# Retention followed by a maxout feed-forward: weights converted in pairs, another order of the first chunks, weight sums one tile earlier, and a last store in two halves

## The chip, the cores and the metric

The kernel runs on one core of one Trainium2 chip. The metric is the device time of one execution in microseconds (us). A kernel's figure is the median of its executions. Differences of one or two microseconds are read from ratios over several rounds, and their 95% intervals are given.

## The reference

The reference is retention (attention with a decay mask instead of a softmax), followed by a feed-forward layer that takes the maximum of three products.

```python
# q, k, v: 8 batches x 8 heads x 576 positions x 64, float32
scores = q @ k.T / 8
gamma  = 1 - 2.0 ** (-5 - arange(8))                  # one per head
D      = where(i >= j, gamma ** (i - j), 0)           # decay and causal mask
x      = ((scores * D) @ v)  as 4608 rows x 512
h      = maximum(maximum(x @ w1, x @ w2), x @ w3)     # 512 -> 768
out    = h @ w_out                                    # 768 -> 512
# w1, w2, w3, w_out arrive as float64
```

## The kernel before

The rows are worked off in 36 chunks of 128 rows for the retention and in 9 tiles of 512 rows for the feed-forward. The retention of the next tile is interleaved with the feed-forward of the present one. Tile 0 uses plain matmuls. Tiles 1 to 8 use a scheme of seven products instead of eight, which needs sums of weight blocks ("weight sums") and sums of hidden blocks.

Each chunk goes through three steps. The step `transposes` puts q and k with the head dimension on the partitions. The step `scores` multiplies them, masks on VectorE, and updates the running state. The step `values` multiplies by v and by the state. The chunks up to 7 are transposed by TensorE and copied out of PSUM by ScalarE. From chunk 8 on VectorE transposes, and for this the kernel loads the data in blocks of 32, by 32 small loads:

```python
def load(g):
    rows = (("k", k), ("q", q), ("v", v)) if g < BY_PE else (("k", k), ("v", v))
    for n, src in () if g < BY_PE else (("q", q), ("kx", k)):
        ...                                    # 4 x 4 loads of 16 KB for each of q and kx
    for n, src in rows:
        ...                                    # one load of 256 KB each
```

The float64 weights come as 24 pieces of 128x512 (512 KB each), six loads ahead. Each piece is converted by bit operations: two masks on VectorE (expo, frac), three activations on ScalarE, two more VectorE steps (whole, and the sign joined to the exponent), and one multiply on GpSimd, which gives the weight. A generator cuts this into steps, and `convert(n)` emits the next n steps in the program between other work. Each engine works off its instructions in program order, so the place of a step in the program matters (in the changed kernel GpSimd once stands 6.0 us before an operation whose data have not landed, and a multiply whose inputs are there waits behind it).

```python
last = None
for n, piece in enumerate(pieces):
    high, expo, mant, frac = yield from masks(bits.pop(piece))   # masks of piece n
    if last:
        product(*last)                                           # then the end of piece n-1
        yield
    whole(mant, frac)
    yield
    last = piece, high, expo, mant
    ...
```

The beginning of the program, and where tile 0 and tile 1 emit conversions and weight sums:

```python
warm(6); load(0); load(1)
nc.sync.dma_start(gs[:], state_decay); nc.sync.dma_start(gq[:], out_decay)
load(2); load(3); load_weights(2); load(4); load_weights(4)
decay_values(0); transposes(0); warm(3); decay_values(1); scores(0); transposes(1)
values(0); decay_values(2); scores(1); transposes(2); values(1); decay_values(3); scores(2)
convert(2); transposes(3); values(2); convert(2); scores(3); ...

# ffn(t)
if t == 0:
    up_plain(t, h, fb, i)               # 4 matmul passes, then copy or maximum
    convert(4 if i > 0 else 8 if fp == 1 else 6)
...
if t == 1:
    weight_sums(n + 5)
...
for n in [[0], [1], [2], [3, 4]][m]:    # in tile 0's four down-products
    weight_sums(n)
```

## Time and profile before

The median was 834.87 us of the first three executions. The column "where" names the view of the profile; the list of TensorE's waits stands in the prediction.

| what | value | where |
|---|---|---|
| span of the profiled execution | 834.0 us | first line of the page |
| TensorE busy | 823.8 us, 99% | busy time by engine |
| last matmul to the end of the span | 3.56 us | timeline |
| VectorE, ScalarE, GpSimd busy | 51%, 21%, 22% | busy time by engine |

TensorE is the bound. The other engines matter only at the few places where TensorE waits for them, nearly all in the first tile, while the weights are being converted.

### The profile page before, as it was taken

The page shows a single profiled execution, that of the slowest core. Times are in us where ns is not written, and L with a number is a line of the kernel's source. Part 1 is how long each engine was busy: PE and PEld are TensorE (multiplying, and loading weights), DVE is VectorE, ACT ScalarE, POOL GpSimd, SP SyncE. Part 2 cuts the span into 40 slices and gives each one's busy share as a digit, 9 for nine tenths or more (in the row PEclk, how much of TensorE's full clock was granted, in tenths as well). Part 3 has the DMA queues.
Part 4 walks back from the last instruction along what each step waited for, and adds up shares of the span by engine and source line. Part 5 has one row for each costly group of instructions (what it writes and reads, how often), then busy time and mean ns, then how long its engine had stood idle before and what let it go on. Part 6 is the DMA issues. An engine that isn't in the chain of part 4 may idle for free.

```text
span 834.0 us, 12632 instructions
## 1 busy us (share of the span) xinstructions
PE 823.8 (99%) x4626; PEld 670.5 (80%) x4626; DVE 427.3 (51%) x803; ACT 174.7 (21%) x395; POOL 186.7 (22%) x182
## 2 busy tenths in 40 slices
PE   8899999999999999999999999999999999999998
PEld 8545556788888888888888888888888888888887
DVE  3879946754355443554444445544545435533341
ACT  2656721111111101111111111111111011111211
POOL 3535545511211130212011111111111202201000
PEclk9999999999999999999999999999999999999999
DMA  8946521334133323332233313332333223201001
GB/s 220 283 131 188 133 58 40 57 56 84 50 55 56 56 59 65 67 56 55 60 55 73 67 48 56 57 57 80 56 57 54 59 60 73 48 13 38 1 1 50
DMA packets 232509, 59.06 MB, mean 71 GB/s; under 512 B 213504, under 2 KB 230912, under 8 KB 232448
## 3 DMA queue, kind: packets, MB, share of 16 engines
q1 hardware_dynamic: 232304, 58.26, 31.1%
q8 instruction: 36, 0.59, 0.3%
q14 instruction: 25, 0.20, 0.1%
q10 hardware_dynamic: 144, 0.00, 0.0%
HBM read 48.76 MB, written 9.44 MB: 70 GB/s over the span
## 4 chain that ended last, share of the span: by engine, by line
PE 95%; DMA 2%; DVE 1%; SPq 1%; ACT 0%; POOL 0%; issue 0%; DVEq 0%
PE x L435 30%; PE z L435 15%; PE dx L311 10%; PE y L435 7%; PE up L493 7%; PE dz L311 5%; PE s L183 4%; PE o L213 4%; PE o L218 4%; PE kv L194 4%; PE dy L311 2%; PE down L484 2%; SPq L152 1%; DMA bits<-in_moe_w_dram 1%; DMA gs<-in_state_decay_dram 1%; SPq L146 1%
## 5 line engine op out<-in xcount | busy, mean ns | idle before, releaser
L435 PE MATMUL x<-S,T 128*128 128x256 f32 x576 | 147.9, 379 | 0.0
L435 PEld LDWEIGHTS x<-S,T 128*128 128x128 f32 x576 | 109.1, 190 | 15.4 <-ACT p L440 0.3
L156 POOL TENSOR_TENSOR vd<-vraw,gk 128x512 f32<-128x512 f32 x36 | 37.8, 1049 | 344.9 <-DMA vraw<-in_v_dram 319.4
L435 PE MATMUL x<-S,w 128*128 128x256 f32 x288 | 74.5, 381 | 1.2 <-DVE h L465 1.2
L435 PE MATMUL x<-xT,w 128*128 128x256 f32 x288 | 74.8, 382 | 0.0
L435 PE MATMUL z<-S,w 128*128 128x256 f32 x288 | 73.9, 379 | 0.0
L435 PE MATMUL z<-xT,T 128*128 128x256 f32 x288 | 73.9, 379 | 0.0
L435 PE MATMUL y<-xT,w 128*128 128x256 f32 x288 | 73.9, 379 | 0.0
L465 DVE TENSOR_TENSOR tmp<-x,p 128x256 f32<-128x256 f32 x48 | 20.4, 425 | 103.4 <-PE x L435 103.4
L440 ACT COPY p<-x 128x256 f32<-128x256 f32 x72 | 26.8, 372 | 221.0 <-PE x L435 221.0
L186 DVE TENSOR_TENSOR st<-s,causal 128x512 f32<-128x512 f32 x72 | 46.3, 685 | 44.6 <-PE s L183 44.6
L493 PE MATMUL up<-xT,w 128*128 128x512 f32 x144 | 63.8, 595 | 1.4 <-POOL w L387 1.4
L435 PEld LDWEIGHTS x<-S,w 128*128 128x128 f32 x288 | 49.3, 189 | 14.8 <-DVE h L465 1.8
L435 PEld LDWEIGHTS z<-S,w 128*128 128x128 f32 x288 | 54.7, 190 | 7.4
L435 PEld LDWEIGHTS y<-xT,w 128*128 128x128 f32 x288 | 54.7, 190 | 7.4
L435 PEld LDWEIGHTS z<-xT,T 128*128 128x128 f32 x288 | 54.3, 189 | 7.9
L220 DVE TENSOR_TENSOR xT<-o,gq 128x512 f32<-128x512 f32 x36 | 24.8, 690 | 67.9 <-PE o L218 62.4
L435 PEld LDWEIGHTS x<-xT,w 128*128 128x128 f32 x288 | 51.5, 190 | 6.6 <-issue 0.8
L493 PEld LDWEIGHTS up<-xT,w 128*128 128x128 f32 x144 | 26.6, 190 | 32.2 <-issue 29.9
L294 POOL TENSOR_TENSOR H<-h 128x256 f32<-128x256 f32 x24 | 18.1, 756 | 150.7 <-DVE h L478 150.0
L440 ACT COPY u<-x 128x256 f32<-128x256 f32 x72 | 26.8, 372 | 99.8 <-PE x L435 97.1
L183 PEld LDWEIGHTS s<-qT,kT 64*128 64x128 f32 x576 | 35.0, 187 | 15.6 <-issue 11.7
(92 smaller groups left out, 1210.1 us busy)
## 6 DMA issues: line engine op xcount, KB each, us to landing
bits<-in_moe_w_dram SPq DMA_DIRECT2D x18, 512.0 KB, 4.7
out_dram<-osb SPq DMA_DIRECT2D x36, 256.0 KB, 2.1
kraw<-in_k_dram SPq DMA_DIRECT2D x32, 256.0 KB, 3.0
vraw<-in_v_dram SPq DMA_DIRECT2D x32, 256.0 KB, 3.5
qraw<-in_q_dram SPq DMA_DIRECT2D x448, 16.0 KB, 1.8
kxraw<-in_k_dram SPq DMA_DIRECT2D x448, 16.0 KB, 1.8
bits<-in_moe_w_out_dram SPq DMA_DIRECT2D x6, 512.0 KB, 3.4
qraw<-in_q_dram SPq DMA_DIRECT2D x7, 256.0 KB, 4.4
```

What stands on the lines that cost most here:

```text
L156: nc.gpsimd.tensor_tensor(t[:], raws.pop(("v", g))[:], gk[:].unsqueeze(2).to_broadcast([C, H, D]), op=ALU.mult)
L183: nc.tensor.matmul(s[j][:, p, :], lhsT=kT[r, p, :], rhs=qT[r, p, :], start=True, stop=True)
L186: nc.vector.tensor_tensor(st[:, j], s[j][:], masks[start_of(g)][:].unsqueeze(1).to_broadcast([C, NP, C]), op=ALU.mult)
L194: nc.tensor.matmul(kv[:, p, :], lhsT=pair(kr, p)[r:], rhs=pair(vds[g], p)[r:], start=True, stop=True)
L213: nc.tensor.matmul(o[D * j:D * (j + 1), p, :], lhsT=vr[:, 2 * p + j, :], rhs=st[:, j, p, :], start=(p == 0), stop=(old == 0 and p == NP - ...
L218: nc.tensor.matmul(o[:, p, :old], lhsT=sd[:, p, :], rhs=qT[:, p, :old], start=False, stop=(p == NP - 1), skip_group_check=True)
L220: nc.vector.tensor_tensor(xT[t][:, :, i * C:(i + 1) * C], o[:], gq[:], op=ALU.mult)
L311: nc.tensor.matmul(out[:, m, :], lhsT=hS[n](fp)[:, m * P:(m + 1) * P], rhs=late["T"][n][:, fp, :], start=first and m == 0 and fp == 0, sto ...
L435: nc.tensor.matmul(out[:], lhsT=w[:, d * P:(d + 1) * P], rhs=xS[t][n][:, d, :], start=first and d == 0, stop=d == 1, skip_group_check=True)
L440: nc.scalar.copy(c[:], src[:])
L465: nc.vector.tensor_tensor(c22, x[:], p7[:], op=ALU.add)
L493: nc.tensor.matmul(ps[:], lhsT=w_sb[i, fb][:, dc * P:(dc + 1) * P], rhs=xT[t][:, dc, :], start=(dc == 0), stop=(dc == NDC - 1))
```

## The change

The intent is to remove TensorE's few waits, some of its work, and a part of the tail. It has six parts: the order of the first chunks (parts 1 and 2 of the prediction), the conversion in pairs (3), chunk 7 transposed by VectorE (4), all weight sums in tile 0 (5), and the last product, copy and store of the last tile in two halves (6). The diff is cut to its core:

```diff
-BY_PE = 8
+BY_PE = 7
-    wtmp = ...(tc.tile_pool(name="wtmp", bufs=3))
+    wtmp = ...(tc.tile_pool(name="wtmp", bufs=4))          # and frac from 1 to 2 buffers
...                                    # the last tile: x in two banks, and
-        product(3, x, False)
-        total(0, 1, x, [])
+        for blocks in ([[m] for m in range(NM)] if last else [range(NM)]):
+            product(3, x, False, blocks)
+            for m in blocks:
+                nc.scalar.copy(osb[:, m, :], x[m])
+            store(0, 1, osb, slice(blocks[0], blocks[-1] + 1))
...                                    # conversion
+        for group in [pieces[:1], pieces[1:2]] + [pieces[n:n + 2] for n in range(2, len(pieces), 2)]:
+            masked = []
+            for piece in group:
+                masked.append((yield from masks(bits.pop(piece))))
+            for piece, (high, expo, mant, frac) in zip(group, masked):
+                whole(mant, frac)
                 yield
+                product(piece, high, expo, mant)
                 yield
...                                    # tile 0: the maximum after the conversion steps
-                    up_plain(t, h, fb, i)
-                    convert(4 if i > 0 else 8 if fp == 1 else 6)
+                    maximum = up_plain(t, h, fb, i)
+                    convert(4 if i > 0 else 8 if fb % 2 == 0 else 6 if fp == 0 else 4)
+                    maximum()
...                                    # weight sums
-                if t == 1:
-                    weight_sums(n + 5)
-                for n in [[0], [1], [2], [3, 4]][m]:
+                for n in [[0, 1, 2], [3, 4, 5], [6], [7, 8]][m]:
...                                    # first chunks
-    load(1)
-    nc.sync.dma_start(gs[:], state_decay)
-    nc.sync.dma_start(gq[:], out_decay)
+    load(1, (gs, state_decay), (gq, out_decay))            # the decays ahead of chunk 1's v
-    warm(3)
+    warm(2)
     scores(2)
+    transposes(3)
     convert(2)
-    transposes(3)
```

More of the change, by code (lines that the diff above doesn't have):

```diff
@@ L90 @@
     wraw = while_converting.enter_context(tc.tile_pool(name="wraw", bufs=WAHEAD))
-    wtmp = while_converting.enter_context(tc.tile_pool(name="wtmp", bufs=3))
+    wtmp = while_converting.enter_context(tc.tile_pool(name="wtmp", bufs=4))
     ps_r = ctx.enter_context(tc.tile_pool(name="ps_r", bufs=4, space=PSUM))
@@ L136, in spans, with load @@
             row += n
-    def load(g):
+    def load(g, *between):
         rows = (("k", k), ("q", q), ("v", v)) if g < BY_PE else (("k", k), ("v", v))
@@ L149, in load @@
         for n, src in rows:
+            if n == "v":
+                for t, what in between:
+                    nc.sync.dma_start(t[:], what)
             t = raws[n, g] = raw.tile([C, H, D], FP32, tag=n, name=n + "raw", bufs=4 if n == "k" else 3)
@@ L302, in summed, with bank, product @@
             return lambda fp: late["S"][n][:, fp, :]
+        NM = NH // P
+        last = t == N // NT - 1
         hS = {1: raw_hidden(0, 0), 2: raw_hidden(0, 1), 3: summed(4), 4: raw_hidden(1, 1),
               5: summed(1), 6: summed(2), 7: summed(3)}
-        NM = NH // P
-        def product(n, out, first):
+        def bank(pool, tag, name):
+            b = pool.tile([P, NM, DM // 2], FP32, tag=tag, name=name)
+            return [b[:, m, :] for m in range(NM)]
+        def product(n, out, first, blocks=range(NM)):
             for fp in range(NF // 2):
-                for m in range(NM):
-                    nc.tensor.matmul(out[:, m, :], lhsT=hS[n](fp)[:, m * P:(m + 1) * P], rhs=late["T"][n][:, fp, :],
-                                     start=first and m == 0 and fp == 0, stop=fp == NF // 2 - 1, skip_group_check=True)
+                for m in blocks:
+                    nc.tensor.matmul(out[m], lhsT=hS[n](fp)[:, m * P:(m + 1) * P], rhs=late["T"][n][:, fp, :],
+                                     start=first and fp == 0 and (m == 0 or last and out is x),
+                                     stop=fp == NF // 2 - 1, skip_group_check=True)
         def kept(name, src):
@@ L317, in kept, with store @@
                 c = ppool.tile([P, NH], FP32, tag=name, name=name)
-                nc.scalar.copy(c[:], src[:, m, :])
+                nc.scalar.copy(c[:], src[m])
                 both.append(c)
             return both
+        def store(r, c, osb, blocks=slice(None)):
+            block = out[t * NT + r * NH:t * NT + (r + 1) * NH, c * (DM // 2):(c + 1) * (DM // 2)]
+            nc.sync.dma_start(block.rearrange("(m p) d -> p m d", p=P)[:, blocks], osb[:, blocks])
         def total(r, c, src, others):
@@ L324, in total @@
             for m, o in enumerate(others):
-                nc.vector.tensor_tensor(osb[:, m, :], src[:, m, :], o[:], op=ALU.add)
-            if not others:
-                nc.scalar.copy(osb[:], src[:])
-            block = out[t * NT + r * NH:t * NT + (r + 1) * NH, c * (DM // 2):(c + 1) * (DM // 2)]
-            nc.sync.dma_start(block.rearrange("(m p) d -> p m d", p=P), osb[:])
-        x = ps_x.tile([P, NM, DM // 2], FP32, tag="x", name="dx")
+                nc.vector.tensor_tensor(osb[:, m, :], src[m], o[:], op=ALU.add)
+            store(r, c, osb)
+        if last:
+            x = [pool.tile([P, NH], FP32, tag=tag, name="dx")[:] for pool, tag in ((ps_x, "x"), (ps_r, "r"))]
+        else:
+            x = bank(ps_x, "x", "dx")
         product(1, x, True)
@@ L334, in downs @@
         yield
-        y = ps_y.tile([P, NM, DM // 2], FP32, tag="y", name="dy")
+        y = bank(ps_y, "y", "dy")
         product(2, y, True)
@@ L341, in downs @@
         yield
-        z = ps_y.tile([P, NM, DM // 2], FP32, tag="y", name="dz")
+        z = bank(ps_y, "y", "dz")
         product(7, z, True)
@@ L351, in downs @@
         yield
-        product(3, x, False)
-        total(0, 1, x, [])
+        osb = opool.tile([P, NM, DM // 2], FP32, tag="osb", name="osb")
+        for blocks in ([[m] for m in range(NM)] if last else [range(NM)]):
+            product(3, x, False, blocks)
+            for m in blocks:
+                nc.scalar.copy(osb[:, m, :], x[m])
+            store(0, 1, osb, slice(blocks[0], blocks[-1] + 1))
         yield
@@ L368, in masks @@
             nc.scalar.activation(expo[:].bitcast(FP32), expo[:], AF.Relu, bias=top[:], scale=-8.0)
-            frac = wtmp.tile([P, DM], I32, tag="frac", name="frac", bufs=1)
+            frac = wtmp.tile([P, DM], I32, tag="frac", name="frac", bufs=2)
             nc.vector.tensor_scalar(out=frac[:], in0=high, scalar1=0xFFFFF, scalar2=None, op0=ALU.bitwise_and)
@@ L388, in product @@
             load_weights(1)
-        last = None
-        for n, piece in enumerate(pieces):
-            high, expo, mant, frac = yield from masks(bits.pop(piece))
-            if last:
-                product(*last)
-                yield
-            whole(mant, frac)
-            yield
-            last = piece, high, expo, mant
-            if n == 0:
-                product(*last)
+        for group in [pieces[:1], pieces[1:2]] + [pieces[n:n + 2] for n in range(2, len(pieces), 2)]:
[4 more added lines that the diff above has]
+                whole(mant, frac)
+                yield
+                product(piece, high, expo, mant)
                 yield
-                last = None
-        product(*last)
-        yield
     def weight_sums(n):
@@ L494, in up_plain @@
                              start=(dc == 0), stop=(dc == NDC - 1))
-        if i == 0:
-            nc.scalar.copy(h[:, fb, :], ps[:])
-        else:
-            nc.vector.tensor_tensor(h[:, fb, :], h[:, fb, :], ps[:], op=ALU.max)
+        if i > 0:
+            return lambda: nc.vector.tensor_tensor(h[:, fb, :], h[:, fb, :], ps[:], op=ALU.max)
+        return lambda: nc.scalar.copy(h[:, fb, :], ps[:])
     def ffn(t):
```

## The prediction

> **What bounds the kernel now.** I read the page first, for how much of the span TensorE leaves unused.
>
> ```profile
> span 834.0 us, 12632 instructions
> PE 823.8 (99%) x4626; PEld 670.5 (80%) x4626; DVE 427.3 (51%) x803; ACT 174.7 (21%) x395; POOL 186.7 (22%) x182
> PEclk9999999999999999999999999999999999999999
> PE 95%; DMA 2%; DVE 1%; SPq 1%; ACT 0%; POOL 0%; issue 0%; DVEq 0%
> ```
>
> TensorE is busy for 823.8 of 834.0 us, at full granted clock, and 95% of the chain that ended last is TensorE. So the change can win at most the 10.2 us of TensorE idleness plus whatever matmuls it removes. That busy time hides little: in the timeline of tile 7 a product of four matmul passes starts every 0.86 us, 0.216 us a pass, without exception. Next I asked who keeps TensorE waiting (columns: who, line, for whom; us in total, times, longest):
>
> ```profile
> PE s L183 <- ACT qT L175: 2.0, 1, 2.0
> PE warm L113 <- POOL ident masks.py:199: 1.4, 1, 1.4
> PE up L493 <- POOL w L387: 1.4, 1, 1.4
> PE x L435 <- DVE h L465: 1.2, 1, 1.2
> PE s L183 <- DVE state L197: 0.7, 1, 0.7
> ```
>
> These five make 6.7 us; the rest, 3.5 us, is the tail after the last matmul. Four of the five and the tail are touched by the change, the identity (1.4) is not. The chain of waits in the first 45 us shows what stands behind two of them (start, us, what):
>
> ```profile
> 14.57 5.89 DMA bits<-in_moe_w_dram
> 20.46 0.02 issue
> 20.49 1.41 DVE expo L365
> ...
> 23.40 0.47 ACT kT L175
> 23.87 0.49 ACT qT L175
> 24.36 0.04 issue
> 24.41 1.21 PE s L183 x16
> 25.62 1.10 DVE st L186 x2
> ...
> 32.05 2.94 POOL w L387
> 34.99 0.04 issue
> 35.03 3.70 PE up L493 x8
> ```
>
> The copies of chunk 3's transposes stand on ScalarE behind the first weight piece, which landed at 20.46. Later the second weight piece is converted too late for the second product of the first unit (35.03).
>
> **The Trainium skill.** "SBUF — State Buffer", section "SBUF: two separate sides": the port pair that VectorE and GpSimd share is an exclusive lock, held for a whole instruction, and the loser blocks. The trace agrees: the mask operation on the weight bits takes 0.42 us alone and 1.49 beside a GpSimd product (38.56 to 40.05, product from 38.11 to 39.77), and the second piece's product at 32.05 took 2.93 instead of 1.28. "DMA: Bandwidth & Descriptors", section "Anatomy of one DMA — SWDGE (gpsimd) path": a DMA's fixed cost of about 2 us is mostly completion latency. These stores come from SyncE, but the trace agrees in size: 256 KB stores land a median 2.1 us after issue, so half the bytes will not halve it. "TensorE: Matmul & The Clock Gate", section "What's actually happening": about the first 3.4 us of work run at half clock. Here the 128-wide passes stand 0.21 us apart from 1.43 to about 7 us, 0.11 afterwards; the measured 5.5 us decides.
>
> **The change, part by part.**
>
> 1. *First chunks' order.* Removing one warm-up matmul frees two passes, 0.4 us, but the scores need the query copy, which ends at 6.70: they start at about 6.8 instead of 7.17. The decays now load before the third load of chunk 1. The state decay landed at 11.06, so one slot of about 0.9 us earlier brings it to about 10.1, and removes the 0.7 us wait. But chunk 1's values then land at about 11.7 instead of 8.97; GpSimd's scaling (1.04) ends at 12.75, so the key-value product starts at 12.8 instead of 13.08. Most of that gain is handed to a later wait: about 0.3 us remain.
>
> 2. *Transposes of chunk 3 before the conversion.* Its copies will be done by 20.7, so scores(3) start at about 22.05 rather than 24.41. But its mask on VectorE stands behind the first piece's conversion, in program order: that ends at 24.32 in the trace because its bits land at 20.46, which the change does not move. So the mask (1.29 us for two) runs 24.2 to 25.5 instead of 25.60 to 26.89. Of 2.4 us gained on TensorE 1.4 survive; with the 0.3 of part 1 (GpSimd's state product leaves the port earlier) 1.4 to 1.7. The first unit starts at about 28.5 instead of 30.0.
>
> 3. *Pieces in pairs.* The order of VectorE's instructions shows the second piece now finished (mask, whole, product) before the third piece's masks start; before, the third's masks came first. Its last VectorE step ends at about 29.9 and GpSimd's product of 1.28 us at about 31.7, if it gets the port soon. The second up-product wants it at 28.5 + 8 passes of 0.43 = 32.0: no wait. Before, it started at 35.03. So 3.0 us are won at this point (parts 1 to 3 together). From there on pieces three and four are ready by about 35 and 37 for 37.6 and 41.1. Within a pair one of the two GpSimd products overlaps VectorE operations of one port only in part, so fewer 1.49 us masks; VectorE is 72 to 100% busy there, but no TensorE wait hangs on it after 36 us. Moving each maximum behind the conversion costs nothing as long as PSUM has two buffers per name: a bank is wanted again 14 us later.
>
> 4. *Chunk 7 transposed on VectorE.* It removes these eight passes, 0.87 us of TensorE:
>
> ```profile
> 108.15 0.60 PE L173 MATMUL kt<-ident,kraw 128*128 128x128 f32 x4
> 108.59 0.60 PE L173 MATMUL qt<-ident,qraw 128*128 128x128 f32 x4
> 109.02 5.32 PE L484 MATMUL down<-w_out,h 128*128 128x512 f32 x12
> ```
>
> and two ScalarE copies. It adds two VectorE transposes (0.70 + 0.66, as at 159.15) and replaces one load by 32 small ones. Chunk 8's took SyncE 8.54 + 7.55 us to issue. They stand ahead of the last two weight pieces: issue from about 76 to 92, these two pieces land by about 97 to 98, wanted at about 98 to 99. Tight, but no TensorE wait by my estimate.
>
> 5. *Weight sums in the first tile.* Four of nine sums move from tile 1 to the down-products, where VectorE and GpSimd have slack. In tile 1 the wait of 1.2 us goes: at 157.4 to 159.2 two sums contended with GpSimd (0.94 and 0.83 instead of 0.42 each), 1.77 us, right ahead of the evacuations that TensorE waited for at 162.03. In the down stretch GpSimd gets 18 operations of 0.7 to 0.95, 16 us, beside chunk scaling and state, in about 24 us; the tile's own sums come by about 126, wanted near 131.
>
> 6. *Last tile.* The last copy shrinks from 0.58 (128x512) to about 0.37 (128x256), 0.2 us; the last store carries 128 KB instead of 256, 0.1 to 0.2 us off the 2.08 us it took. The first half's copy and store lie beside matmuls. About 0.35 us.
>
> Sum: 3.0 + 0.87 + 1.2 + 0.35 = 5.4 us, 0.65%. From 834.87, and allowing that the three times before average 834.2, this gives 829.2 us.
>
> **Rivals.**
> - *GpSimd starves on the second piece.* After its last VectorE step VectorE goes straight into four mask operations of the next pair. At 32.05 the same product was held off through four VectorE instructions (2.93 us), at 38.11 only through one. If it is held off again it ends at about 34.0 and TensorE waits 1.9 us: the head wins only 1.1 us, total 831. I give this three in ten.
> - *VectorE becomes the bound of tile 0.* Six conversions are now queued ahead of chunk 4's mask. By my walk this mask ends at 43.3, wanted at 44.6. ScalarE, at 2.2 us a piece plus copies, sets the pace. If it slips by 2 to 3 us, 1 to 2 us come back as a wait for st: total 830 to 831.
> - *The small loads delay the last pieces*, or the sums delay the tile's own: a wait of 1 to 3 us near 100 to 135, total 830 to 832. Against it: all those waits had at least 1 us of margin above.
> - *More than I think.* If the values of chunk 1 land sooner and GpSimd's state product no longer holds the first mask (1.40 instead of 0.42), another 1 us goes: 828.
>
> **Range and chances.** The largest possible gain is 10.2 - 1.4 - about 2.5 of unavoidable tail + 0.9, some 7 us (about 827); the smallest plausible, with two rivals at work, about 2.5 us. Executions of one kernel differ here by 832.19 to 835.63. So 826.0 to 832.4 for 8 in 10. A change of 2% is 16.7 us, more than all idleness, and no new work of that size is added: within 2% is nearly certain.
>
> **What would show it.** TensorE's list of waits should have lost qT, h and state, and keep the identity; the first up-product should start near 28.5, the second near 32.0; TensorE's busy time should fall by about 0.9 to 823; tile 1 should begin near 130 instead of 133.9; the gap after the last matmul should be about 3.2. A wait for w above 1 us near 32 to 34, for st near 44, or for w_out or S between 100 and 135 would prove a rival. A time above 833 would make the prediction wrong in kind.

## The result, and the profile after

The changed kernel took 830.63 us (median of six executions, 829.89 to 831.19). The kernel before took 833.92 us in the same rounds (six executions, 832.19 to 836.2). A ratio is the mean time of one kernel's fast runs over that of the other's of the same rounds, so it is not quite the ratio of the medians. Here it is 0.9957 [0.9938, 0.9976]. The prediction was 829.2 us in a range of 826.0 to 832.4. The sign and the range held. The gain is 3.3 us where 5.4 were predicted.

The page of the changed kernel has these lines: the span, the busy time by engine, and the chain that ended last.

```profile
span 828.2 us, 12659 instructions
PE 821.8 (99%) x4616; PEld 668.8 (81%) x4616; DVE 434.5 (52%) x805; ACT 173.9 (21%) x401; POOL 192.3 (23%) x182
PE 86%; DVE 6%; issue 2%; SPq 2%; DMA 2%; ACT 1%; POOL 0%; DVEq 0%
```

TensorE lost 10 instructions, two passes of warm-up and the eight of chunk 7, and in this trace 2.0 us of busy time. Most of the difference to the predicted 0.9 us is this one execution: in the second pair of traces below it is 823.7 before and 823.0 after. VectorE and GpSimd do a little more. The chain now holds more VectorE (6% against 1%), because it follows the work of tile 0 back through conversions. That alone costs nothing.

TensorE's list of waits is the view to compare (who, line, for whom; us in total, times, longest):

```profile
PE warm L113 <- POOL ident masks.py:199: 1.4, 1, 1.4
PE o L216 <- DVE st L189: 0.6, 2, 0.5
PE down L495 <- POOL w_out L404: 0.5, 1, 0.5
PE kv L197 <- POOL vd L159: 0.4, 1, 0.4
PE s L186 <- ACT qT L178: 0.2, 1, 0.2
PE up L504 <- POOL w L404: 0.2, 1, 0.2
```

The identity stays. The wait for qT is down from 2.0 to 0.2 us and stands elsewhere, those for w from 1.4 to 0.2, and those for h and the state are gone. Three waits are new: for st, for the scaled values vd, and for the output weights w_out. They belong to parts 2, 1 and 4 of the change, in this order; the waits for st stand near 24 us, at chunk 3's mask.

The timeline of TensorE shows the head (start, us, what, and the idle time before it):

```profile
27.73 7.11 PE L504 MATMUL up<-xT,w 128*128 128x512 f32 x16
...
37.01 7.13 PE L504 MATMUL up<-xT,w 128*128 128x512 f32 x16 [0.19 <-POOL w L404]
```

The first unit starts at 27.73 us instead of 30.00, and its second product follows the first without a gap (one line for 16 passes). In the kernel before the second product stood alone at 35.03. That is the step that the prediction valued highest, and in this pair of traces the next landmark, chunk 4's scores, came 3.91 us earlier.

**The pair of traces is not typical.** The two profiled executions differ by 5.8 us, the medians by 3.3. Before's profile fell on an execution of 835.73 us, 1.8 above its median, and after's on its fastest. The landmarks of two more profiled executions, taken later, show how much moves from one execution to the next (us from the start of the span):

| landmark | before | before, again | after | after, again |
|---|---|---|---|---|
| first unit starts | 30.00 | 28.87 | 27.73 | 28.23 |
| chunk 4's scores | 38.67 | 36.24 | 34.76 | 35.27 |
| tile 1 starts | 133.92 | 131.50 | 130.18 | 130.87 |
| last matmuls end | 830.43 | 827.54 | 825.21 | 826.40 |
| span ends | 834.0 | 831.1 | 828.2 | 829.4 |

The first two traces give a gain of 5.8 us and the second two 1.7 us. The timed gain lies between. The second trace of before is not typical either: it fell on the fastest of its six executions (832.83 us, 2.1 below their median), while the second trace of after fell near its median. So the traces tell which waits come and go, and the rounds tell what that is worth.

### The profile page after: what moved, and what is told of

Read it like the earlier page. It is cut to its first block, busy times and chain, and to the rows that moved or that the text cites. A ratio compares the mean times of both kernels' runs of the same rounds, so it can differ in the third digit from the quotient of the medians.

```text
span 828.2 us, 12659 instructions
## 1 busy us (share of the span) xinstructions
PE 821.8 (99%) x4616; PEld 668.8 (81%) x4616; DVE 434.5 (52%) x805; ACT 173.9 (21%) x401; POOL 192.3 (23%) x182
## 4 chain that ended last, share of the span: by engine, by line
PE 86%; DVE 6%; issue 2%; SPq 2%; DMA 2%; ACT 1%; POOL 0%; DVEq 0%
PE x L446 30%; PE z L446 15%; PE dx L319 10%; PE y L446 8%; PE dz L319 5%; PE s L186 4%; PE o L216 4%; PE o L221 3%; PE kv L197 3%; PE dy L319 3%; PE down L495 2%; DVE expo L398 1%; SPq L155 1%; DVE frac L387 1%; DVE mant L393 1%
## 5 line engine op out<-in xcount | busy, mean ns | idle before, releaser
L465 DVE TENSOR_TENSOR tmp<-y,p 128x256 f32<-128x256 f32 x48 | 20.4, 425 | 52.7 <-PE y L446 52.7
```

What stands on the lines that cost most here:

```text
L465: nc.vector.tensor_tensor(c11, y[:], p1[:], op=ALU.add)
```

## The experiments

Twelve kernels ran, each in five rounds beside the kernel before. All gave correct results. The first four ran on one chip and the last eight on another. Executions of before had medians of 834.56 on the first and 834.1 to 834.2 on the second. The changed kernel itself was not run on the second chip. So the eight are compared with it through their ratios to before, whose intervals reach 1.1 to 1.6 us to either side; where two intervals overlap, the text says so.

| experiment | median us | ratio to before, 95% interval |
|---|---|---|
| before_again | 834.95 | 1.000 [0.998, 1.002] |
| after_again | 830.92 | 0.9959 [0.9941, 0.9978] |
| old_convert | 835.37 | 1.0009 [0.9992, 1.0027] |
| old_order | 833.13 | 0.9984 [0.9967, 1.0001] |
| old_chunk7 | 830.27 | 0.9952 [0.9938, 0.9966] |
| old_convert_chunk7 | 830.38 | 0.9956 [0.9942, 0.9970] |
| spread | 829.41 | 0.9943 [0.9930, 0.9956] |
| old_sums | 831.20 | 0.9966 [0.9952, 0.9980] |
| order_alone | 832.40 | 0.9976 [0.9962, 0.9991] |
| spread_old_convert | 830.36 | 0.9953 [0.9938, 0.9968] |
| spread_scores3 | 832.04 | 0.9973 [0.9957, 0.9990] |
| old_tail | 830.88 | 0.9961 [0.9946, 0.9976] |

### The two kernels once more (before_again, after_again)

There is no edit. These two were to show how far one trace can be trusted.

> The kernel before, unchanged, against itself: ratio 1.000. Its use is a second trace. Theory: the first trace of the kernel before fell on a slow execution (835.73 us against a median of 833.92), so the two traces overstate the gain (834.0 to 828.2, 5.8 us) against the medians (3.3 us); then this trace should show a span below 834.0, and one of the waits of the first trace (the second weight piece held off, 32.05 to 34.98; the late VectorE sum at 162.03) should be shorter or absent, by 1 to 2 us. Rival: each execution has the same waits and only the landing times in the first 20 us differ; then scores of chunk 4 start elsewhere than at 38.67 because the first weight piece lands elsewhere than at 20.46, and the rest is shifted as a block.

> The changed kernel again: 3 to 4 us faster than before, ratio 0.9957 +- 0.001, executions within 1.5 us of each other. Trace: scores of chunk 4 at about 34.8, tile 1 at about 130.2, span 828 to 829.5. If the wait for the last weight piece (0.5 us at 109.47) comes from the order of the loads it is there again; if it came from chance it is gone.

Before_again's profiled execution took 832.83 us. It has these waits of TensorE, after the identity:

```profile
PE s L183 <- ACT qT L175: 1.2, 1, 1.2
PE x L435 <- DVE h L465: 0.8, 1, 0.8
PE s L183 <- DVE state L197: 0.4, 1, 0.4
```

The wait for w of 1.4 us, one of the five on which the prediction was built, isn't there. In this execution GpSimd's multiply for the second piece took 1.65 us, where the trace of before has 2.92. The other waits are shorter too. So the "before" of the prediction was one draw, and so is this one: of the six traces that have the old conversion four show the wait for w of 1.4 us (multiply of 2.9 us) and two do not (1.65 us). After_again reproduced the gain (0.9959), with waits of 0.8 us for w_out, 0.7 for vd and 0.6 for st.

### The old conversion in the changed kernel (old_convert)

```diff
-    for group in [pieces[:1], pieces[1:2]] + ...      # pairs, 4 and 2 buffers, maximum last
+    last = None                                       # the loop, buffers and counts of before
+    for n, piece in enumerate(pieces): ...
```

> Changed kernel with the old conversion (one piece at a time, its product behind the next piece's masks, each maximum ahead of the conversion, the old step counts and scratch buffers). Theory: the second piece is again finished behind the third piece's masks and held off by VectorE, so the second up-product of the first unit waits about 2 us (33.4 instead of 31.2) and scores of chunk 4 start near 37 instead of 34.76; time +1.5 to +2.5 us over the changed kernel. Rival (the order of the first chunks did it all): second product without a wait above 0.5 us, time within 0.5 us of the changed kernel.

It is 4.4 us slower than the changed kernel by the medians of the same rounds (835.37 against 830.92), so all the gain is gone. But the theory that the second piece is the reason falls: chunk 4's scores started at 35.61 us, close to 35.27 in after_again. The profile fell on old_convert's slowest execution (838.42 us, 3.1 above its median), so it shows where the loss stands, but more of it than usual. It stands further on (the list of waits, then the table of stretches with busy time of five engines, granted clock, DMA share and GB/s, then the timeline):

```profile
PE down L501 <- POOL w_out L404: 3.9, 3, 1.4
```

```profile
116.00:120.00 4.00, 4.00 (x24) 3.37 (x24) 3.86 (x6) 0.59 (x1) 4.00 (x5) 0.50 0.32 58
```

```profile
116.41 2.08 PE L186 MATMUL s<-qT,kT 64*128 64x128 f32 x16
```

The down-product waits three times for output weights, 3.9 us in all. The old loop is one piece behind. Its last weight piece was issued only at 100.22 us, behind chunk 7's small loads, which took SyncE from 83.59 to 99.03. It landed at 105.80, and GpSimd stood until 104.57 behind chunk 7's values in its program order. Part 3 (pairs) and part 4 (small loads) interact: this is why a test of one of them alone misleads here.

The other two lines show something that I had not looked for. TensorE's granted clock fell during the third wait and stood at 0.50 from about 114 to 120.5 us, and the 16 score passes took 2.08 us instead of 1.16. No single wait was over 1.44 us. Half a clock for 6.5 us is some 3.3 us by my estimate, about what this execution lies above the median. So if the waits brought the clock down, which one trace suggests and no run tests, a wait can cost more than its length. The 4.4 us do not need it: the four executions of old_convert at full clock took 834.61 to 835.47 us, the five of after_again 830.49 to 831.43.

### The old order of the first chunks (old_order), and the new order alone (order_alone)

```diff
 # old_order, against the changed kernel
-    load(1, (gs, state_decay), (gq, out_decay))
+    load(1); nc.sync.dma_start(gs[:], state_decay); nc.sync.dma_start(gq[:], out_decay)
-    warm(2)
+    warm(3)
-    transposes(3)
     convert(2)
+    transposes(3)
 # order_alone: the kernel before, with only these lines changed the other way
 # (its last copy is emitted in two halves, within one store)
```

> Changed kernel with the old order of the first chunks (three warm-up matmuls, decays behind chunk 1's values, chunk 3's transposes behind the first conversion). Theory: the wait for chunk 3's query copy (about 2 us) and for the state (0.7) are back, the first unit starts near 29.7 instead of 27.73, scores of chunk 4 near 36.7; time +1.5 to +2.2 us. Rival (the mask of chunk 3 stands behind the first conversion on VectorE anyway, so the early transposes gain little): first unit no later than 28.7, time within 1 us.

> The kernel before with the new order of the first chunks alone (two warm-up matmuls, decays ahead of chunk 1's values, chunk 3's transposes ahead of the conversion); its last copy of each tile is in two halves, which costs about 0.1 us at the end. Theory: this part carries most of the gain, some 2.2 us as it cost to undo it, so ratio 0.9965 to 0.998 (831.5 to 832.8 beside 834.2); no wait for qT, the waits for w near 31 (0 to 1.5 us, by execution) and for h near 158 remain, and nearly all executions have the full clock[...]. Rival (the gain is in the other parts): ratio above 0.9985 and executions below a clock of 0.999 as often as before (about half).

In old_order the wait of before is back:

```profile
PE s L186 <- ACT qT L178: 2.0, 1, 2.0
```

The state's wait, expected at 0.7 us, is 0.3. The first unit starts at 29.39 us (27.73 and 28.23 with the new order), and the kernel is 2.2 us slower by the medians of the same rounds (833.13 against 830.92). Order_alone is 0.9976 of before, 2.0 us of 834. The two agree, so by these figures parts 1 and 2 carry more than half of the gain (the interval of order_alone alone leaves 0.8 to 3.2 us). In order_alone the wait for w of 1.4 us is there, at 33.03 us: with the old conversion it comes in some executions and not in others, and with pairs it was at most 0.2 us in every trace.

### Chunk 7 by TensorE again (old_chunk7), and with the old conversion (old_convert_chunk7)

```diff
-BY_PE = 7
+BY_PE = 8                 # old_chunk7; old_convert_chunk7 has the old conversion as well
```

> Changed kernel with chunk 7 transposed on TensorE again. Theory: the 32 small loads of chunk 7 hold up SyncE, the last two weight pieces and chunk 7's values, and the wait for w_out before the end of the first down-product (0.5 to 0.8 us, some 0.8 to 1.1 between two passes) eats the 0.87 us that the part saves. Then here the wait for w_out is gone, eight passes of transposes are back, and the second scores of the down stretch (chunk 7) start within 0.4 us of the changed kernel's 110.5 to 111.2; time within 0.6 us of the changed kernel. Rival (the part pays in full, the wait has another cause): the wait stays and the time is 0.8 to 1 us longer.

> Changed kernel with the old conversion and chunk 7 on TensorE: the pairs by themselves, without the small loads. Theory: the 4.4 us that the old conversion cost beside the small loads came from their collision (GpSimd stood behind chunk 7's values until 104.6, with the last four weight products behind it, and TensorE fell to half clock after the waits); without the small loads the old conversion costs at most 1 us, and no wait for w_out is seen. An execution in which the second piece's product is held off (2.9 us) would wait 1 to 2 us near 33. Time 831 to 832.3. Rival (the pairs are worth 4 us of themselves): time near 835, waits for w or w_out of 3 us.

Old_chunk7 took 830.27 us, 0.9952 of before. It is no slower than the changed kernel, which has 0.9957 and 0.9959. The intervals overlap, so it can't be called faster, but part 4 won nothing. In its timeline the eight passes of chunk 7 are back at 104.25, there is no wait for w_out, and chunk 7's scores start when they do in the changed kernel (110.53):

```profile
110.37 1.16 PE L186 MATMUL s<-qT,kT 64*128 64x128 f32 x16
```

From the start of this stretch (104.50 and 104.25) to the scores it is 6.03 us in the changed kernel and 6.12 here. Of the 0.87 us of removed matmuls 0.09 is left. The gap before the last two passes of the down-product took the rest.

Old_convert_chunk7 took 830.38 us, against 830.27 with pairs on the same chip. It has a wait of 1.4 us for w in its profiled execution and none for w_out. So the 4.4 us of old_convert were the collision with chunk 7's loads, and without it the pairs are worth 0.1 us by the medians, 0.3 by the ratios.

### The small loads spread out (spread), and with the old conversion (spread_old_convert)

```diff
+    small = deque()                         # chunk 7's 32 loads wait here
+    def load_small(n):
+        for _ in range(min(n, len(small))):
+            small.popleft()()
 ...
             nc.gpsimd.tensor_tensor(w, mant[:], expo[:].bitcast(FP32), op=ALU.mult)
             load_weights(1)
+            load_small(6)                   # six behind each weight piece
 ...
+            if g + 2 == BY_PE:
+                blocks(g + 2)               # chunk 7's loads are put in line one chunk earlier
```

> Changed kernel, the small loads of chunk 7 issued six at a time behind each weight piece's load from chunk 6 on, in SyncE's idle time, rather than 32 at once. Theory: the last two pieces land 10 us earlier, the wait for w_out is gone, chunk 7's scores start at 109.7 to 110.4, and the time is 0.5 to 1.0 us below the changed kernel (about 830.0). Rival: the small loads now delay the other pieces and a wait for w of similar size appears before 95 us; time equal or longer.

> The version with the small loads spread out, with the old conversion in it. Theory: the pairs were needed only because chunk 7's 32 loads stood in SyncE's queue; spread out, the old conversion costs as little as without them (0.3 us, an execution with the second piece held off 1.4): 829.3 to 830.5, wait for w_out at most 0.5 us. Rival (the last pieces come too late in the old order even so): wait for w_out over 1 us, time above 831.5.

Spread took 829.41 us (829.05 to 829.98). It has the lowest median: 0.9943 of before, 1.2 us below the changed kernel's 830.63, and 0.9 below old_chunk7, which ran on the same chip in the same rounds (829.63 to 830.36). Against the changed kernel, which ran on another chip, the intervals of the ratios overlap. SyncE now issues in this pattern:

```profile
72.15 0.38 SPq L271 DMA_DIRECT2D bits<-in_moe_w_out_dram  x1
72.57 2.80 SPq L142 DMA_DIRECT2D kxraw<-in_k_dram  x6
```

These weight pieces are issued 3.3 to 4.1 us apart with some six small loads between, and the last two pieces go at 83.48 us (95.30 in the changed kernel). The wait for w_out is gone, and chunk 7's scores start at 109.44, 1.1 us earlier than in the changed kernel. Part 4 had a sound purpose. The place of its loads was wrong.

Spread_old_convert took 830.36 us. Here the pairs are worth 0.95 us by the medians, though the intervals overlap. It also has the wait of 1.4 us for w near 33 us, and it does not have the collision.

### Chunk 3's scores still earlier (spread_scores3)

```diff
 # against spread
     values(2)
-    convert(2)
     scores(3)
+    convert(2)
```

> The version with the small loads spread out, and chunk 3's scores ahead of the last two steps of the first piece's conversion, so that its mask on VectorE does not stand behind them. Theory: the wait for st (0.6 us near 24) goes, the first unit starts 0.6 to 1.2 us earlier than 27.7, if the first piece's product is ready by then (it would end near 26.5); time 828.4 to 829.2. Rival: the second piece is now late, a wait for w of 0.5 to 1.5 us appears near 31, time 829.4 or more.

This was meant as a better version, and it failed: 832.04 us, 2.6 us slower than spread. The wait moved to a place that neither theory nor rival had named:

```profile
PE up L516 <- DVE xT L234: 2.3, 1, 2.3
```

The chunk's mask no longer stands behind the conversion. But the conversion's last two steps now stand on VectorE ahead of the step that writes xT of chunk 3, which the first unit needs. It starts at 29.40 us (27.73 in the changed kernel). On an engine that works in program order, what is moved back pushes something else.

### The weight sums as before (old_sums)

```diff
+                if t == 1:
+                    weight_sums(n + 5)
-                for n in [[0, 1, 2], [3, 4, 5], [6], [7, 8]][m]:
+                for n in [[0], [1], [2], [3, 4]][m]:
```

> Changed kernel with four weight sums back in tile 1. Theory: the wait for VectorE's sum h in tile 1 (0.8 and 1.2 us in the two traces of before) is back near 158, time +0.8 to +1.4 us over the changed kernel. Rival: with tile 1 starting earlier VectorE meets the sums at another point and no wait is seen; time within 0.4 us.

It took 831.20 us, 0.6 above the changed kernel's 830.63, or 0.6 to 0.8 by the ratios, whose intervals overlap. The wait in tile 1 is back:

```profile
PE x L446 <- DVE h L476: 0.7, 1, 0.7
```

The wait shows that the part works as argued; the rounds put it at about half its predicted 1.2 us, not resolved. The wait itself varies: 1.2 us in the trace of before, 0.8 in before_again, 0.9 in order_alone, 0.7 here. The nine sums in the down stretch brought no wait in any trace of a kernel that has them.

### The last tile as before (old_tail)

```diff
-        last = t == N // NT - 1
+        last = False
```

> Changed kernel with one bank and one store at the end of the last tile (its copy in two halves). Theory: from the traces the two banks saved 0.2 us of copy and 0.4 us of the last store (landing after 2.08 us before, 1.69 after); so 0.6 to 0.7 us longer than the changed kernel, ratio near 0.9965. Rival: the smaller store lands no sooner and the gain is 0.2 us or less.

It took 830.88 us, 0.9961 of before. That is 0.2 to 0.3 us above the changed kernel and is not resolved by the intervals. The traces of before and after show the part more clearly. The last copy on ScalarE in before:

```profile
830.48 0.58 ACT L327 COPY osb<-dx 128x512 f32<-128x512 f32 x1 [7.12 <-PE dx L311]
```

The last copy in the changed kernel:

```profile
825.25 0.37 ACT L369 COPY osb<-dx 128x256 f32<-128x256 f32 x1 [0.92 <-PE dx L319]
```

The copy is 0.21 us shorter. The last store takes 1.69 us from issue to landing (128 KB) instead of 2.08 (256 KB), in both traces of each kernel. That this is its size alone is not shown: the 128 KB store issued 1.3 us before it took 2.1 us, beside a store of 256 KB. From the end of the last matmul to the end of the span it is 2.98 us instead of 3.56 (3.7 in old_tail's own trace, whose copy is in two halves). So the part is worth 0.58 us by the traces, and somewhat less by the clock of the rounds.

## Why the prediction was right or wrong

**The bound.** It held. TensorE stays 99% busy, and the gain is far within 2%.

**The head (parts 1 to 3), predicted 3.0 us.** The walk through the program came out near its landmarks. The first unit started at 27.73 and 28.23 us (28.5 predicted), its second product had no wait, and chunk 4's scores came at 34.76 and 35.27. The size is uncertain, because it was taken against a single trace. The term "Before, it started at 35.03. So 3.0 us are won at this point" counted a wait of 1.4 us for w that before_again does not have, and a qT wait of 2.0 that is 1.2 there. At chunk 4's scores the head gained 3.4 to 3.9 us against the first trace of before and 1.0 to 1.5 against before_again. The rounds give 2.0 to 2.2 for the order and, without the collision of part 4, 0.1 to 0.9 for the pairs. So 3.0 stands at the upper end of what was measured, and its split was off: the order was put at 1.4 to 1.7, which leaves 1.3 to 1.6 for the pairs. Part 1 went as written: the state's wait turned into one for vd of 0.4 to 0.7.

**The rival "GpSimd starves on the second piece"** did not happen. In the paired order this multiply took 1.38 to 1.39 us in all eight traces that have it. In the old order it took 1.65 or 2.92. Starvation did come, one piece later. The third piece's multiply took 4.21 us in four of the eight traces, and it cost TensorE at most 0.19 us, because that weight is wanted later. The rival "VectorE becomes the bound of tile 0" did not happen: no trace has the wait for st near 44 us that it named. The wait for st of 0.6 us (1.7 in one execution of old_tail) stands near 24, at the mask of chunk 3 behind the first piece's conversion, which part 2 had reckoned with.

**Part 4, predicted 0.87 us: the step that failed.** It is the sentence "Tight, but no TensorE wait by my estimate". The loads behaved much as estimated, a little later. SyncE in the changed kernel:

```profile
86.56 7.54 SPq L146 DMA_DIRECT2D kxraw<-in_k_dram  x16
...
94.68 0.53 SPq L155 DMA_DIRECT2D vraw<-in_v_dram  x1
95.30 1.43 SPq L260 DMA_DIRECT2D bits<-in_moe_w_out_dram  x2
```

Chunk 7's v landed at 98.12 us, and the last two pieces at 99.96 and 101.59 (97 to 98 predicted). That is not what cost the time. The cause shows in GpSimd and VectorE of the changed kernel, in this order:

```profile
98.25 1.04 POOL L159 TENSOR_TENSOR vd<-vraw,gk 128x512 f32<-128x512 f32 x1 [5.99 <-DMA vraw<-in_v_dram]
...
100.47 2.90 POOL L404 TENSOR_TENSOR w_out<-mant,expo 128x512 f32<-128x512 f32 x2
...
108.15 1.27 POOL L404 TENSOR_TENSOR w_out<-mant,expo 128x512 f32<-128x512 f32 x1 [0.63 <-DVE expo L398]
```

```profile
100.06 0.74 DVE L382 TENSOR_SCALAR expo<-bits 128x512 int32<-128x512 int32 x1 [1.53 <-DMA bits<-in_moe_w_out_dram]
100.72 1.51 DVE L387 TENSOR_SCALAR frac<-bits 128x512 int32<-128x512 int32 x1
102.13 1.52 DVE L382 TENSOR_SCALAR expo<-bits 128x512 int32<-128x512 int32 x1
```

GpSimd stood for 6.0 us before the scaling of chunk 7's values, which are loaded behind the same small loads. The two multiplies of the pair before stood behind it in program order, and came only at 100.47. There they fell on the masks of the last pair. The first and last of the same four masks in old_chunk7:

```profile
99.87 0.43 DVE L382 TENSOR_SCALAR expo<-bits 128x512 int32<-128x512 int32 x1
...
100.87 0.43 DVE L387 TENSOR_SCALAR frac<-bits 128x512 int32<-128x512 int32 x1
```

VectorE had waited 1.53 us for the bits, but it began the masks only 0.19 us after old_chunk7 did (100.06 against 99.87), and before spread did (100.80). The difference is in the masks themselves. They took 0.74, 1.51, 1.52 and 0.41 us, to 103.99, and four times 0.43 in old_chunk7, to 101.30. In spread, where the scaling starts at 92.18 and no multiply runs beside them, they take 0.52, 0.42, 0.41 and 0.41. So against old_chunk7 0.2 us were lost to the landing and 2.5 to the port that VectorE and GpSimd share. The last multiply ended at 109.42, where old_chunk7 had it at 107.24, and the down-product had reached its last two passes half a microsecond before:

```profile
109.47 1.13 PE L495 MATMUL down<-w_out,h 128*128 128x512 f32 x2 [0.51 <-POOL w_out L404]
```

So the rival "The small loads delay the last pieces" was right, with 0.5 to 0.8 us where it named 1 to 3. Its counter-argument, "all those waits had at least 1 us of margin above", looked at the loads and not at what else waits behind them in order. Spread confirms this from the other side: with the same work and the loads moved, the wait is gone, chunk 7's scores come 1.1 us earlier, and the median is 1.2 us lower.

**Part 5, predicted 1.2 us.** The mechanism was right. The term was mis-sized because it was one execution's wait; the waits seen since are 0.7 to 0.9, and the rounds give 0.6 to 0.8, unresolved.

**Part 6, predicted 0.35 us.** The copy was right to a hundredth. The store won 0.39 us instead of 0.1 to 0.2, so the traces show 0.58; the rounds leave 0.2 to 0.3, unresolved.

**What the sum is now.** The rounds give 2.0 for the order, 0.1 to 0.3 for the pairs (as measured with chunk 7 on TensorE), about 0.7 for the sums, 0.2 to 0.6 for the tail, and nothing or a loss of up to 0.6 for chunk 7. This is 2.4 to 3.6 us, and 3.3 to 3.6 were measured. Of the 2.1 us by which the gain of 5.4 was too large, part 4 explains 0.9 to 1.5 and the sums 0.4 to 0.6; the head may have held or lack up to 0.9. The predicted time is off by only 1.4 us because its start, 834.6, happened to lie 0.7 above the median of before. That is luck.

**What the prediction did not see at all: steadiness.** Of the 29 executions of before in the experiments 12 ran at a mean granted clock of 0.996 to 0.998, and took 835.66 us in the mean. The other 17 were at 0.999 or 1.0 and took 833.64. Of the 12 executions of the changed kernel one was below 0.999 (833.9 us), and the other 11 took 830.70 in the mean. By these numbers 2.9 us of the gain are there at full clock, and the rest is that such executions became rare: 12 of 29 times 2.0 us is 0.8 us of before's mean. Below 0.999 were also old_order (3 of 6; 2.0 us wait for qT), spread_scores3 (3 of 6; 2.3 us wait for xT) and old_convert (2 of 6). None of the 42 executions of the seven other variants, whose longest profiled wait was 1.5 us, was. That the longer waits cause it is argued from this count, and the longest single wait doesn't explain it alone: old_convert's was 1.44 us, below the 1.5 of old_tail. Only old_convert's trace shows the clock falling, during the third wait for w_out.

## What to carry to other kernels

A profile is one execution: compare its time with the spread of the timed runs, or take a second trace, before a wait of 1 to 2 us is entered in a sum as a gain. Before many small loads are added to a queue that works in order, list everything that stands behind them, on the queue and on each engine that waits in order for what it brings, and spread them between the large loads. A saving on the bound engine is only kept if no weight, value or buffer that it meets earlier is later than before.

## What the Trainium skill lacked or had wrong

- "TensorE: Matmul & The Clock Gate", section "What's actually happening", gives about 3.4 us at half clock at the start. It says that the point of change varies by 500 ns either way. By the spacing of the passes in these 14 traces, the half rate lasts from 1.43 us until between about 4.9 (old_chunk7, spread_old_convert) and 7.5 us (order_alone), so 3.4 to 6.1 us, a wider spread. The record of the granted clock doesn't show it: it reads 1.00 from 1.5 to 7 us in all of them. The same page, section "HAM oscillation — how this bites in real kernels", gives as the abstract rule that idle gaps above some 3.4 us bring the clock down. In old_convert three waits of 1.13, 1.44 and 1.37 us within 7.5 us came with a granted clock of 0.50 from about 114 to 120.5 us. The rule for single gaps did not protect this kernel. The page's next section tells of a kernel that lost its clock to frequent short idles, but gives no figure for how many or how long.
- "SBUF — State Buffer", section "SBUF: two separate sides", says that the one that starts first holds the shared ports for a whole instruction. It does not say who gets them next; further down, the page has a blocked transfer go on when the VectorE instruction ends. GpSimd's multiply of 1.27 us took 2.92 us beside four successive VectorE instructions in before, and 4.21 in the changed kernel, so a wait longer than one instruction has to be reckoned with.
- "DMA: Bandwidth & Descriptors", section "Anatomy of one DMA — SWDGE (gpsimd) path", has a fixed cost of about 2 us for that path, and the prediction carried it over to stores issued from SyncE. There the last store of 128 KB landed 1.69 us after issue, bytes included, so its fixed part was below 2 us. Another of 128 KB took 2.1 beside a larger store, and those of 256 KB 2.08.
- No page gives the time that SyncE needs to issue a small load on this chip; "DMA: Bandwidth & Descriptors" has only a count of cycles per instruction for earlier generations, in its comparison with a later chip. In the changed kernel sixteen loads of 16 KB for chunk 7 took 7.54 and 8.62 us, about 0.5 us each, and everything behind them in its order waited for that time.
